# Two attention blocks on one core: an order of instructions laid out by a model of four engines, scores of four heads in one burst, transposes moved off the tensor engine, and a new start

## The chip, the cores and the metric

The kernel runs on one core of one Trainium2 chip. The metric is the device time in microseconds (us) of one execution on that core. Five engines work side by side, each through its own queue in program order: PE (tensor engine, matmuls), ACT (scalar engine, here the exponentials), DVE (vector engine), POOL and SP. SP does no arithmetic here; it issues all DMAs through one queue. PE's products go to PSUM, which both kernels lay out as eight banks of 512 f32 columns. To "evacuate" a bank is to copy it out, mostly by DVE, so that it can be used again. The "chain" of a profile is the work that ended last, followed back from wait to wait.

## The reference, cut to what matters

Two attention blocks read their own input of 2048 rows and 640 columns, and their outputs are put side by side. Both have 32 heads of 20 columns.

```python
# A: four segments of 512 rows; inside a segment causal attention, plus a memory M, z
for s in range(4):
    p = softmax(qs @ ks.T * 20 ** -0.5 + mask)          # per head
    a_dot = p @ vs
    a_mem = (phi(qs) @ M) / (phi(qs) @ z + 1e-6)        # phi(t) = t + 1 if t > 0 else exp(t)
    o = g * a_mem + (1 - g) * a_dot                     # g = sigmoid(beta), per head
    M = M + phi(ks).T @ vs;  z = z + phi(ks).sum(rows)
out_A = o @ wo
# B: sliding window, each row sees itself and the 255 rows before it
out_B = (softmax(q @ k.T * 20 ** -0.5, window 256) @ v) @ wo
```

Both kernels cut the work into eight chunks of 512 rows and run A0, B0, A1, B1, A2, B2, A3, B3. While one chunk's scores and exponentials run, the next chunk's q, k and v are projected.

## The kernel before

Four heads lie in four blocks of 32 partitions (20 used). A "slot" is one pair of heads and one block of keys and queries: two score matmuls on two row tiles of PE (a row tile is 32 of its 128 rows, used by itself), then one exp.

```python
    def bank(self):                                   # small PSUM banks: four
        return self.ps.tile([P, 512], F32, name="m", bufs=4)

    def scores(self, banks, b, pair, g, k, q, koff):  # L329, L336
        ps = self.ps.tile([P, 2, 512], F32, name="sc", bufs=2)
        for kt, q0, nq, c0 in banks[b]:
            for i in range(2):
                rows = slice(HD * (2 * pair + i), HD * (2 * pair + i) + HD)
                nc.tensor.matmul(ps[:, i, c0:c0 + nq * P], lhsT=k[rows, g, kc:kc + P],
                                 rhs=q[rows, g, q0 * P:(q0 + nq) * P], ...
                                 tile_position=(HD * (2 * pair + i), 0))
        nc.scalar.activation(out=pt[:, :, lo:hi], in_=ps[:, :, lo:hi], func=ACT.Exp, ...)
```

The product of probabilities and values (AV) comes out with the head's columns on partitions and has to be turned. DVE first copies it out of PSUM, PE turns it, DVE normalises. The finished rows are turned a second time for the output projection, again on PE.

```python
    def evac(self, O):                                # L409
        oc = self.wk.tile([P, 512], BF16, name="oc", bufs=4)
        self.nc.vector.tensor_copy(out=oc[:], in_=O[:])
    def turn(self, oc):                               # L415
        for b in range(LT):
            self.nc.tensor.transpose(out=t[:, b * P:(b + 1) * P],
                                     in_=oc[:, b * P:(b + 1) * P], identity=self.ident[:])
    def final_job(self, o_tok, b, wo, out_rows):      # L440 to L454
        for m in range(self.KT):
            nc.tensor.transpose(out=t[:, m * P:(m + 1) * P],
                                in_=o_tok[:, b, m * P:(m + 1) * P], identity=self.ident[:])
        nc.vector.tensor_copy(out=oT[:], in_=t[:, 0:self.KT * P])
        ...                                           # 2 x 5 matmuls with wo, copy, store
```

The next chunk's q and k take a round trip through memory so that heads land on blocks of 32 partitions: `st` is stored to scratch (`scr_qB<-st`), then read back by head ("spread", `qB<-scr_qB`). A class `Filler` hands out the projections between the slots by a credit that counts PE time only. The start fills large tiles with zeros on POOL while DVE computes the gate constants.

The softmax here doesn't subtract the row's maximum and nothing guards it: scores larger than these inputs give would overflow.

Of the kernel before, what the change touches and what calls it, by code (L numbers as in the profile page):

```python
# [2 lines left out]

# [5 lines left out]
ACT = mybir.ActivationFunctionType  # L9
# [13 lines left out]
VW = H * VS + 12  # L23
EPS = 1e-6

BANKS_A = [[(0, 0, 4, 0)], [(3, 3, 1, 0), (1, 1, 3, 128)], [(2, 2, 2, 0)]]
BANKS_B = [[(-2, 0, 1, 0), (0, 0, 3, 128)], [(2, 2, 2, 0), (-1, 0, 2, 256)],
           [(3, 3, 1, 0), (1, 1, 3, 128)]]
BANKS_B0 = [[(0, 0, 3, 128)], [(2, 2, 2, 0)], [(3, 3, 1, 0), (1, 1, 3, 128)]]
# [6 lines left out]
class Filler:  # L36

    def __init__(self, nslots):
        self.jobs = deque()
        self.nslots = nslots  # L40
        self.credit = 0.0

    def add(self, deadline, cost, gen):
        self.jobs.append([deadline, cost, gen])

    def step(self):
        job = self.jobs[0]
        try:
            c = next(job[2])
            job[1] = max(0.0, job[1] - c)  # L50
            return c
        except StopIteration:
            self.jobs.popleft()
            return 0.0

    def force(self, t):
        while any(j[0] <= t for j in self.jobs):
            self.credit -= self.step()

    def run(self, t, extra):  # L60
        total = sum(j[1] for j in self.jobs)
        rate = total / max(1, self.nslots - t)
        cum = 0.0
        for d, c, _ in self.jobs:
            cum += c
            rate = max(rate, cum / max(1, d - t))
        self.credit = min(self.credit + rate + extra, 1500.0)
        while self.jobs and self.credit > 0:
            self.credit -= self.step()

    def drain(self):
        while self.jobs:
            self.step()


class _K:

    def __init__(self, ctx, tc, S, D):
        self.ctx, self.tc, self.nc = ctx, tc, tc.nc
        self.S, self.D = S, D  # L80
        self.KT = D // P
        self.scale = float(DH) ** -0.5

# [9 lines left out]
    def bank(self):  # L93
        return self.ps.tile([P, 512], F32, name="m", bufs=4)

    def bank16(self):
        return self.ps.tile([P, 1024], BF16, name="m", bufs=4)
# [15 lines left out]
    def consts_masks(self):  # L113
        nc, cp = self.nc, self.cp
        self.zero = nc.gpsimd.to_reg(0.0)
        ident = cp.tile([P, P], BF16, name="ident")
        nc.gpsimd.memset(ident[:], 0.0)
        nc.gpsimd.affine_select(out=ident[:], in_=ident[:], pattern=[[-1, P]],
                                compare_op=ALU.not_equal, fill=1.0, base=0,
                                channel_multiplier=1)  # L120
        self.ident = ident
# [11 lines left out]
        self.rowmask = rowmask[:, 0:1]  # L133
        epsv = cp.tile([P, 1], F32, name="epsv")
        nc.vector.tensor_scalar(out=epsv[:], in0=rowmask[:],
# [17 lines left out]
    def consts_beta(self, beta):  # L153
        nc, cp = self.nc, self.cp
        b = cp.tile([P, H], BF16, name="beta")
        nc.sync.dma_start(out=b[:], in_=beta.rearrange("(o n) -> o n", o=1).to_broadcast([P, H]))
        e = cp.tile([P, H], F32, name="e32")
        nc.scalar.activation(out=e[:], in_=b[:], func=ACT.Exp, scale=-1.0)
        t = cp.tile([P, H], F32, name="t32")
        nc.vector.tensor_single_scalar(out=t[:], in_=e[:], scalar=1.0, op=ALU.add)  # L160
        r = cp.tile([P, H], F32, name="r32")
        nc.vector.reciprocal(out=r[:], in_=t[:])
        omg = cp.tile([P, H], F32, name="omg")
        nc.vector.tensor_tensor(out=omg[:], in0=e[:], in1=r[:], op=ALU.mult)
        self.omg = omg
        g8 = cp.tile([P, G], F32, name="g8")
        ev = e[:].rearrange("p (g j) -> p g j", j=4)
        for j in range(4):
            rows = slice(HD * j, HD * j + HD)
            nc.vector.tensor_copy(out=g8[rows, :], in_=ev[rows, :, j])  # L170
        self.g8 = g8

    def proj_direct(self, w, xT, dst, g, mask):
        nc = self.nc
        ps = self.bank()
        for kt in range(self.KT):
            for j in range(4):
                c0 = DH * (4 * g + j)
# [4 lines left out]
            yield mm_ns(512)  # L183
        if mask:
# [4 lines left out]
        yield 0.0  # L189

    def proj_compact(self, w_ap, xT, st, phi=None):
        nc = self.nc
        for m in range(self.KT):
            ps = self.bank()
            for kt in range(self.KT):
# [3 lines left out]
                yield mm_ns(512)  # L199
            nc.vector.tensor_copy(out=st[:, m, :], in_=ps[:, :])  # L200
            yield 0.0

    def spread(self, dst, src, c0, n, d0=0):
        for j in range(4):
            self.nc.sync.dma_start(
                out=dst[HD * j:HD * j + DH, :, d0:d0 + n],
                in_=src[:, c0:c0 + n].rearrange("(g j d) s -> j d g s", g=G, j=4)[j])

    def qk_job(self, w_ap, xT, scratch, col, dst, c0, n, d0=0):
        st = self.wk.tile([P, self.KT, L], BF16, name="st", bufs=2)  # L210
        yield from self.proj_compact(w_ap, xT, st)
        self.nc.sync.dma_start(
            out=scratch[:, col:col + L].rearrange("(m p) s -> p m s", p=P), in_=st[:])
        self.spread(dst, scratch, c0, n, d0)
        self.last_st = st
        yield 0.0

    def pq_job(self, scratch, dst):
        nc = self.nc
        st = self.last_st  # L220
        pc = self.wk.tile([P, self.KT, L], BF16, name="pqc", bufs=1)
        for m in range(self.KT):
            self.phi(pc[:, m, :], st[:, m, :])
            yield 250.0
        nc.sync.dma_start(out=scratch[:, :].rearrange("(m p) s -> p m s", p=P), in_=pc[:])
        self.spread(dst, scratch, 0, L)
        yield 0.0

    def phi(self, out, in_):
        nc = self.nc  # L230
        e = self.wk.tile([P, L], BF16, name="e", bufs=2)
        nc.scalar.activation(out=e[:], in_=in_, func=ACT.Exp)
        nc.vector.tensor_single_scalar(out=e[:], in_=e[:], scalar=1.0, op=ALU.min)  # L233
        nc.vector.scalar_tensor_tensor(out=out, in0=in_, scalar=0.0, in1=e[:],  # L234
                                       op0=ALU.max, op1=ALU.add)

    def pk_job(self, src, nt, pkT):
        nc = self.nc
        pend = None
        for i in range(nt + 1):  # L240
            if i < nt:
                pk = self.wk.tile([P, L], BF16, name="pk", bufs=2)
                self.phi(pk[:], src[:, i, :])
                yield 250.0
            if pend is not None:
                pi, ppk = pend
                pt = self.bank16()
                for b in range(LT):
                    nc.tensor.transpose(out=pt[:, b * P:(b + 1) * P],
                                        in_=ppk[:, b * P:(b + 1) * P],  # L250
                                        identity=self.ident[:])
                yield 4 * mm_ns(128)
                nc.vector.tensor_copy(
                    out=pkT[:, :, pi * P:(pi + 1) * P],
                    in_=pt[:, 0:LT * P].rearrange("p (b c) -> p b c", b=LT))
                yield 0.0
            pend = (i, pk)

    def dm_job(self, seg, pkT, coloff, v):
        nc = self.nc  # L260
        dM = self.bank()
        dv = dM[:, 0:G * HD].rearrange("p (g c) -> p g c", c=HD)
        for g in range(G):
            for kt in range(LT):
                for j in range(4):
                    h = 4 * g + j
                    rows = slice(HD * j, HD * j + HD)
                    nc.tensor.matmul(dv[rows, g, 0:VS],
                                     lhsT=pkT[:, kt, coloff(h):coloff(h) + HD],
# [3 lines left out]
                yield 4 * 27.0  # L273
# [8 lines left out]
        self.mz = mz  # L282
        MZ = self.wk.tile([P, G, HD], BF16, name="MZ", bufs=2)
# [5 lines left out]
        self.MZ = MZ  # L289
        yield 0.0  # L290

    def v_job(self, w_ap, xT, v, gate):
        nc = self.nc
        for tt in range(LT):
            for hf in range(2):
                ps = self.bank()
                for kt in range(self.KT):
# [3 lines left out]
                    yield mm_ns(320)  # L301
# [10 lines left out]
                yield 0.0  # L312

    def v_tile(self, name, n):
        out = []
        for i in range(n):
            v = self.big.tile([P, LT, VW], BF16, name="%s%d" % (name, i))
            self.nc.gpsimd.memset(v[:], 1.0)
            out.append(v)
        return out  # L320

    def scores(self, banks, b, pair, g, k, q, koff):
        nc = self.nc
        ps = self.ps.tile([P, 2, 512], F32, name="sc", bufs=2)
        for kt, q0, nq, c0 in banks[b]:
            for i in range(2):
                rows = slice(HD * (2 * pair + i), HD * (2 * pair + i) + HD)
                kc = P * (kt + koff)
                nc.tensor.matmul(ps[:, i, c0:c0 + nq * P], lhsT=k[rows, g, kc:kc + P],  # L329
                                 rhs=q[rows, g, q0 * P:(q0 + nq) * P],  # L330
                                 start=True, stop=True,
                                 tile_position=(HD * (2 * pair + i), 0))
        lo = min(e[3] for e in banks[b])
        hi = max(e[3] + e[2] * P for e in banks[b])
        pt = self.wk.tile([P, 2, 512], BF16, name="pt", bufs=12)
# [347 lines left out]
```

## Time and profile before

| before | |
|---|---|
| median (range, runs) | 530.2 us (527.1 to 531.0, 16) |
| span of the profiled run, granted PE clock | 528.5 us, 0.906 |
| first matmul, first exp | 8.9 us, 27.4 us |
| end of the last exp, end | 509.5 us, 528.5 us |
| chunks, first exp to first exp | 63.3, 63.2, 54.0, 71.1, 54.2, 73.2, 54.2, 48.8 us |

Four lines of the page: the DMA queue (packets, MB, share of the time of 16 DMA engines), and the groups of exps and scores (line, engine, operation, output<-input, shapes, count | busy us, mean ns of one | idle time of that engine just before them, and what ended most of it).

```profile
q1 hardware_dynamic: 52136, 40.32, 28.3%
...
L336 ACT ACTIVATE pt<-sc 128x1024 bf16<-128x1024 f32 (+2 forms) x384 | 346.4, 929 | 128.6 <-PE sc L329 115.6
...
L329 PE MATMUL sc<-qB,kB 32*128 32x128 bf16 (+2 forms) x704 | 79.5, 303 | 8.8 <-ACT pt L336 8.0
L329 PE MATMUL sc<-qA,kA 32*128 32x128 bf16 (+3 forms) x512 | 67.7, 304 | 14.9 <-DVE qA L188 14.3
```

The DMA engines are busy for little more than a quarter of the time. Score matmuls hold PE for 79.5 + 67.7 = 147 us of busy time, and ACT stands idle for 128.6 us in front of its exps.

### The profile page before, as it was taken

The page shows a single profiled execution, that of the slowest core. Times are in us where ns is not written, and L with a number is a line of the kernel's source. Part 1 is how long each engine was busy: PE and PEld are TensorE (multiplying, and loading weights), DVE is VectorE, ACT ScalarE, POOL GpSimd, SP SyncE. Part 2 cuts the span into 40 slices and gives each one's busy share as a digit, 9 for nine tenths or more (in the row PEclk, how much of TensorE's full clock was granted, in tenths as well). Part 3 has the DMA queues.
Part 4 walks back from the last instruction along what each step waited for, and adds up shares of the span by engine and source line. Part 5 has one row for each costly group of instructions (what it writes and reads, how often), then busy time and mean ns, then how long its engine had stood idle before and what let it go on. Part 6 is the DMA issues. An engine that isn't in the chain of part 4 may idle for free.

```text
span 528.5 us, 11841 instructions
## 1 busy us (share of the span) xinstructions
PE 451.8 (85%) x4781; PEld 202.1 (38%) x4806; DVE 331.3 (63%) x690; ACT 364.7 (69%) x419; POOL 261.0 (49%) x530
## 2 busy tenths in 40 slices
PE   3099998699798999969899899878979899899965
PEld 0043334333244334434344334433334433444433
DVE  0845555845656767766666677775674677766643
ACT  0046678667787777867878677775877777879950
POOL 9623344356564344635555344544544444468850
PEclk9689999569799999968979999995987999979988
DMA  8900234103541154100563035300262105301101
GB/s 244 344 8 2 51 98 112 42 2 92 157 101 39 43 143 104 39 14 2 151 146 80 27 100 125 74 29 1 76 154 71 40 14 125 100 14 38 39 14 50
DMA packets 52191, 41.07 MB, mean 78 GB/s; under 512 B 22440, under 2 KB 51496, under 8 KB 52136
## 3 DMA queue, kind: packets, MB, share of 16 engines
q1 hardware_dynamic: 52136, 40.32, 28.3%
q8 instruction: 37, 0.61, 0.5%
q14 instruction: 18, 0.15, 0.1%
HBM read 18.69 MB, written 16.38 MB: 66 GB/s over the span
## 4 chain that ended last, share of the span: by engine, by line
PE 70%; DVE 14%; ACT 7%; issue 3%; POOL 0%; POOLq 0%; ACTq 0%; DVEq 0%
PE sc L329 18%; PE m L196 15%; PE m L298 9%; PE m L450 9%; PE m L391 8%; ACT pt L336 6%; PE m L415 4%; PE m L179 3%; DVE oT L444 2%; DVE pk L234 2%; DVE ot L454 2%; DVE oc L409 1%; DVE pqc L234 1%; DVE e L233 1%; PE m L403 1%
## 5 line engine op out<-in xcount | busy, mean ns | idle before, releaser
L336 ACT ACTIVATE pt<-sc 128x1024 bf16<-128x1024 f32 (+2 forms) x384 | 346.4, 929 | 128.6 <-PE sc L329 115.6
L342 POOL TENSOR_SCALAR_AFFINE_SELECT pt<-pt 128x256 bf16<-128x256 bf16 (+1 forms) x336 | 165.9, 497 | 215.6 <-ACT pt L336 213.9
L348 POOL TENSOR_SCALAR_AFFINE_SELECT pt<-pt 128x256 bf16<-128x256 bf16 x176 | 81.2, 463 | 33.0 <-ACT pt L336 33.0
L409 DVE CAST oc<-m 128x512 bf16<-128x512 f32 x88 | 58.5, 688 | 55.7 <-PE m L391 54.2
L329 PE MATMUL sc<-qB,kB 32*128 32x128 bf16 (+2 forms) x704 | 79.5, 303 | 8.8 <-ACT pt L336 8.0
L329 PE MATMUL sc<-qA,kA 32*128 32x128 bf16 (+3 forms) x512 | 67.7, 304 | 14.9 <-DVE qA L188 14.3
L200 DVE CAST st<-m 128x512 bf16<-128x512 f32 x70 | 48.1, 688 | 26.3 <-PE m L196 23.9
L196 PE MATMUL m<-xT,wB 128*128 128x512 bf16 x185 | 51.6, 381 | 1.6 <-issue 1.0
L454 DVE CAST ot<-m 128x320 bf16<-128x320 f32 x64 | 31.3, 489 | 29.9 <-PE m L450 29.3
L329 PEld LDWEIGHTS <-kA 32*128 32x128 bf16 x512 | 19.2, 91 | 73.0 <-issue 55.5
L329 PEld LDWEIGHTS <-kB 32*128 32x128 bf16 x704 | 22.9, 94 | 58.5 <-issue 53.0
L450 PEld LDWEIGHTS <-oT 128*128 128x128 bf16 x320 | 26.2, 100 | 40.4 <-DVE oT L444 21.3
L450 PE MATMUL m<-wo_B,oT 128*128 128x320 bf16 x160 | 31.2, 322 | 8.2 <-DVE oT L444 7.8
L298 PEld LDWEIGHTS <-xT 128*128 128x128 bf16 x320 | 28.2, 105 | 22.5 <-issue 11.7
L450 PE MATMUL m<-wo_A,oT 128*128 128x320 bf16 x160 | 31.1, 302 | 6.3 <-DVE oT L444 6.3
L298 PE MATMUL m<-wv_A,xT 128*128 128x320 bf16 x160 | 35.8, 363 | 0.0
L415 PE MATMUL m<-ident,oc 128*128 128x128 bf16 x352 | 32.6, 230 | 3.6 <-DVE oc L409 3.6
L362 DVE TENSOR_TENSOR pt<-pt,fdmask 128x512 bf16<-128x512 bf16 x48 | 21.9, 457 | 19.0 <-ACT pt L336 18.4
L429 DVE TENSOR_TENSOR o_tok<-m,rr 128x320 bf16<-128x320 bf16 x64 | 31.5, 492 | 2.2
L391 PE MATMUL m<-pt,vB 128*32 128x384 bf16 (+2 forms) x704 | 29.2, 301 | 1.9 <-POOL pt L348 1.9
L298 PE MATMUL m<-wB,xT 128*128 128x320 bf16 x160 | 28.4, 301 | 0.0
L426 DVE RECIPROCAL rr<-m 128x16 f32<-128x16 bf16 x88 | 22.2, 252 | 8.2 <-PE m L415 7.3
(68 smaller groups left out, 417.0 us busy)
## 6 DMA issues: line engine op xcount, KB each, us to landing
out_dram<-ot SPq DMA_DIRECT2D x32, 160.0 KB
kB<-scr_kB SPq DMA_DIRECT2D x12, 240.0 KB
scr_kB<-st SPq DMA_DIRECT2D x4, 640.0 KB
scr_qB<-st SPq DMA_DIRECT2D x4, 640.0 KB
qB<-scr_qB SPq DMA_DIRECT2D x16, 160.0 KB
wB<-in_B_wqkv_dram SPq DMA_DIRECT2D x1, 2400.0 KB
scr_kA<-st SPq DMA_DIRECT2D x3, 640.0 KB
kA<-scr_kA SPq DMA_DIRECT2D x12, 160.0 KB
```

The lines of the kernel that those rows point to most:

```text
L196: nc.tensor.matmul(ps[:, :], lhsT=w_ap[:, kt, m * P:(m + 1) * P], rhs=xT[:, kt, :], start=(kt == 0), stop=(kt == self.KT - 1))
L200: nc.vector.tensor_copy(out=st[:, m, :], in_=ps[:, :])
L298: nc.tensor.matmul(ps[:, 0:320], lhsT=xT[:, kt, tt * P:(tt + 1) * P], rhs=w_ap[:, kt, 320 * hf:320 * hf + 320], start=(kt == 0), stop=(kt ...
L329: nc.tensor.matmul(ps[:, i, c0:c0 + nq * P], lhsT=k[rows, g, kc:kc + P], rhs=q[rows, g, q0 * P:(q0 + nq) * P], start=True, stop=True, tile ...
L336: nc.scalar.activation(out=pt[:, :, lo:hi], in_=ps[:, :, lo:hi], func=ACT.Exp, scale=self.scale)
L342: self.nc.gpsimd.affine_select(out=blk, in_=blk, pattern=[[0, 2 * n], [1, P]], compare_op=ALU.is_ge, fill=self.zero, base=0, channel_multi ...
L348: self.nc.gpsimd.affine_select(out=blk, in_=blk, pattern=[[0, 2], [-1, P]], compare_op=ALU.is_ge, fill=self.zero, base=-1, channel_multipl ...
L391: nc.tensor.matmul(O[HD * j:HD * j + HD, q0 * P:(q0 + nq) * P], lhsT=v[:, vt, VS * h:VS * h + HD], rhs=pts[(b, j // 2)][:, j % 2, c0:c0 + ...
L409: self.nc.vector.tensor_copy(out=oc[:], in_=O[:])
L415: self.nc.tensor.transpose(out=t[:, b * P:(b + 1) * P], in_=oc[:, b * P:(b + 1) * P], identity=self.ident[:])
L450: nc.tensor.matmul(ps[:, 0:320], lhsT=oT[:, m * P:(m + 1) * P], rhs=wo[:, m, 320 * hf:320 * hf + 320], start=(m == 0), stop=(m == self.KT ...
L454: nc.vector.tensor_copy(out=ot[:, 320 * hf:320 * hf + 320], in_=ps[:, 0:320])
```

## The change

The change has four parts. The second and the third take work off PE; the first lays out the order so that all engines are fed.

1. **Order.** `Filler` goes. A class `Flow` keeps a clock for PE, ACT, DVE and POOL while the program is built, with a duration for each kind of instruction, and at each step issues what its model says is ready. As with `Filler`, the order is fixed once the program is built; nothing is decided on the chip.
2. **Scores.** Four heads in one burst on four row tiles, into two score tiles. Three score tiles (six banks) in place of two, so two small banks in place of four. Half-width blocks of A are joined in pairs (384 exps become 352).
3. **Transposes.** AV is turned by DVE straight out of PSUM, in blocks of 32x32, with no copy before. Heads are regrouped (h = 8j + g) so that this gives rows. The turn for the output projection becomes four stores to scratch and one transposing DMA back. The keys for the memory go the same way. The last chunk multiplies its padded heads by a padded weight instead, with the evacuation shared between ACT and DVE.
4. **Start.** Zero fills on DVE as 32-bit words, the gate constants later.

```diff
-class Filler:
-    ...                       # credit per slot, counts PE time only
+class Flow:
+    def __init__(self):
+        self.pe = self.act = self.dve = self.pool = 0.0
+        self.bank_free = [0.0, 0.0]
+    def on_pe(self, mode, ns, ready=0.0):
+        if mode != self.mode:
+            ns += 110.0       # another tile shape
+            self.mode = mode
+        self.pe = max(self.pe, ready) + ns
+        return self.pe
+    ...
     def bank(self):
-        return self.ps.tile([P, 512], F32, name="m", bufs=4)
+        f.pe = max(f.pe, f.bank_free.pop(0))
+        return self.ps.tile([P, 512], F32, name="m", bufs=2)
...
-        ps = self.ps.tile([P, 2, 512], F32, name="sc", bufs=2)
-        for kt, q0, nq, c0 in banks[b]:
-            for i in range(2):
+        ps = [self.ps.tile([P, 2, 512], F32, name="sc", bufs=NSC) for _ in range(2)]   # NSC = 3
+        for g, kt, q0, nq, c0 in ent:
+            for j in range(4):
...
-    def evac(self, O):
-        oc = self.wk.tile([P, 512], BF16, name="oc", bufs=4)
-        self.nc.vector.tensor_copy(out=oc[:], in_=O[:])
-    def turn(self, oc):
-        for b in range(LT):
-            self.nc.tensor.transpose(...)
+    def turn(self, O, tt, i):
+        self.nc.vector.transpose(out=tt[:, i, :], in_=O[:, :])
...
     def final_job(...):
-        for m in range(self.KT):
-            nc.tensor.transpose(...)
-        nc.vector.tensor_copy(out=oT[:], in_=t[:, 0:self.KT * P])
+        for j in range(4):
+            nc.sync.dma_start(
+                out=scr[:, GW * j:GW * (j + 1)].rearrange("(b t) c -> t b c", t=HD),
+                in_=o[HD * j:HD * (j + 1), :, :])
+        yield t + 4500.0
+        oT = self.big.tile([P, self.KT, L], BF16, name="oT", bufs=2)
+        nc.sync.dma_start_transpose(out=oT[:], in_=scr[:, :])
+        yield max(t + 4500.0, f.pe) + (14000.0 if n < 7 else 6000.0)
...
-        nc.gpsimd.memset(qB[:], 0.0)
-        nc.gpsimd.memset(kB[:], 0.0)
+        nc.vector.memset(self.qB[:].bitcast(F32), 0.0)
+        nc.vector.memset(self.kB[:].bitcast(F32), 0.0)
```

## The prediction

> **What bounds the kernel now.** I read the page first: busy shares, chain, then the waits.
>
> ```profile
> PE 451.8 (85%) x4781; PEld 202.1 (38%) x4806; DVE 331.3 (63%) x690; ACT 364.7 (69%) x419; POOL 261.0 (49%) x530
> ...
> PE 70%; DVE 14%; ACT 7%; issue 3%; POOL 0%; POOLq 0%; ACTq 0%; DVEq 0%
> ```
>
> The tensor engine (PE) carries 70% of the chain that ended last, the scalar engine (ACT) only 7%. The list of waits (total us, times, longest) says who waits for whom:
>
> ```profile
> ACT pt L336 <- PE sc L329: 115.6, 198, 13.2
> ...
> PE sc L329 <- DVE qA L188: 14.3, 2, 13.5
> ...
> PE sc L329 <- ACT pt L336: 8.0, 13, 1.7
> ```
>
> ACT waits 115.6 us for scores; PE waits 8.0 us for ACT. So PE is the bound between start and tail. The timeline of PE alone (start, duration, ..., count) shows how it spends itself:
>
> ```profile
> 200.18 0.85 PE L298 MATMUL m<-wB,xT 128*128 128x320 bf16 x5
> 200.97 0.39 PE L329 MATMUL sc<-qA,kA 32*128 32x512 bf16 x2
> 201.29 0.85 PE L298 MATMUL m<-wB,xT 128*128 128x320 bf16 x5
> ...
> 203.50 0.73 PE L391 MATMUL m<-pt,vA 128*32 128x512 bf16 x16
> 204.16 0.40 PE L403 MATMUL m<-pqA,MZ 32*32 32x512 bf16 x4
> ```
>
> Durations overlap, so I count from start to start. Five 320-column matmuls take 0.79 us (200.18 to 200.97); inside such a run the step is 0.136 us (320 columns at 2.4 GHz plus 2.5 ns), five are 0.68, so about 0.1 us goes to the change to another tile shape. Two 512-column score matmuls on two row tiles take 0.32 us: 0.213 once (they run side by side) plus 0.1. Sixteen L391 matmuls (four heads, 1280 columns each) take 0.66 us, 0.53 plus 0.1: four column tiles do run side by side.
>
> The ends: the first scores wait, and the last exp is at 509.5 of 528.5 us.
>
> ```profile
> 14.26 7.61 DVE L160 TENSOR_SCALAR t<-e 128x32 f32<-128x32 f32 x1 [11.95 <-ACT e L158]
> 18.32 3.51 POOL L488 MEMSET pqA<- 128x4096 bf16 x1
> ...
> 26.75 0.62 PE L329 MATMUL sc<-qA,kA 32*128 32x512 bf16 x4 [13.54 <-DVE qA L188]
> ...
> 524.98 0.49 DVE L454 CAST ot<-m 128x320 bf16<-128x320 f32 x1 [0.19 <-PE m L450]
> ```
>
> A 32-element vector (DVE) instruction took 7.61 us and ends with the pool engine's memset (21.87 against 21.83 us), with the first evacuations queued behind it.
>
> **What the Trainium skill says.** "TensorEngine Tiling (Array Packing)", Key Properties: changing the tiling mode drains the engine. The trace agrees, about 0.1 us a change. "TensorE: Matmul & The Clock Gate", Measured speedup vs the span model: four 32-row tiles run together, 3.07 times faster measured, each a few ns behind the other. The trace shows it for four column tiles and for pairs of row tiles; four row tiles no run shows yet. "Advanced Engine Details and Errata", Mode Summary: the second vector port is shared with GpSimd and the two block each other. The 7.61 us above fits. "VectorE: DVE Perf Modes", The three transpose paths: the vector transpose works in 32x32 blocks only; its time for 128x512 from PSUM no run shows. I take that of the evacuation of equal size, 0.69 us long, 0.60 to 0.61 from start to start when back to back.
>
> **The change part by part.** I counted PE instructions in the program order of both kernels and priced them start to start: columns/2.4 ns plus 2.5, divided by the tiles side by side, plus 0.1 us per change of tile shape.
>
> Scores: four heads in one burst over two score buffers, where there were two. 1216 matmuls stay; 77 us become 40. PE transposes go: 352 (L415), 160 (L440) and 72 (L249) at 0.056 us are 33 us. Their work moves to DVE (32x32 blocks out of PSUM, 88 times), and to transposing DMAs through DRAM (7 outputs, 3 keys). The last chunk instead multiplies padded heads by a padded weight: output projection 43.5 becomes 46.7 us. Changes of tile shape: 789 become 415, 79 us become 41. All else on PE (projections, values, AV, memory: 185 us) stays. PE floor: 417 before, 314 after, **103 us less**.
>
> ACT: the half-width score blocks of A are joined, 384 exps become 352. A run of 15 full exps took 13.86 us, so 0.92 each; 320 x 0.92 + 16 x 0.71 + 16 x 0.50 + 33 x 0.52 = 331 us, plus 1.4 for four copies in the tail: 332, about as before. So ACT, now waiting, becomes the longer of the two.
>
> DVE: evacuation of oc, copies to oT and pkT go (88 x 0.60 + 32 x 0.40 + 18 x 0.33 = 72 us), 88 transposes (53) and 8 in the tail come, normalisation takes about as long as before. 331 busy become about 280.
>
> PE and ACT limit different chunks, so I cut both orders at the chunk boundaries. In us, PE/ACT: A0 55/41, B0 35/39, A1 35/37, B1 41/49, A2 36/37, B2 39/47, A3 41/37, B3 33/46. The larger of each pair sums to **350 us**.
>
> Start: the first matmul came at 8.92 us, waiting for weights, and does not move. The wait of 13.5 us should vanish: the large zero memsets leave POOL for DVE in uint32 form, ahead of the first evacuations, and the beta constants run late. Add about 4 us for the cold clock (five 512-column steps took 0.43 us each at the start instead of 0.22). Tail: 19 us after the last exp become about 10, by my sum: mask 0.4, AV 0.7, transpose to transpose on DVE 1.9, some 30 matmuls of 0.14 = 4, evacuation 0.5, last store 3 (525.5 to 528.5 now).
>
> Sum without losses: 8.9 + 4 + 350 + 10 = 373.
>
> Losses: before, PE's floor without the tail is about 408 us and the stretch from first matmul to last exp, less the start wait, 487: a factor of 1.19. The clock row has a mean of 0.906, that is about 100 us at half speed, 15 of it at the start; where PE is the bound those cost some 43 us; without them the factor is 1.09. The slow windows lie where PE does transposes and waits for DVE (0.66 in 88 to 118 us); without PE transposes I expect few. I take 1.08 on 350, 28 us: **about 402 us**.
>
> **The rivals.** (1) *ACT bubbles.* Three score buffers hold one and a half bursts: burst i+1 can start only when the first exp of burst i is done, and must be written within the 0.92 us of the second. An AV of 0.7 us in the way starves ACT. For: queues are in program order, so a drift is not made good. Against: PE steps are 0.14 to 0.22 us and the order was laid out with durations that the trace confirms. 0.3 us on half of 176 bursts is 26 us: 400 with little else, 425 with DVE stalls. (2) *DVE as the bound.* The small PSUM pool shrinks from four banks to two, and every projection, AV and memory product needs one. For: 280 us of DVE in 390 is 72%, and norms now read two SBUF operands, contending with POOL. Against: PE waited 0.6 us only for oc with four banks, and DVE is below 80% in any chunk by count. It would make 430 to 450. (3) *DMA round trips late.* Queries and keys went from store to first use in about 10.5 us (79.85 to 90.3); the last projection of the next chunk is 10 to 19 us of PE work before the boundary. Added output round trips share the one in-order queue. A miss of 3 us at each of seven boundaries is 21 us: 420. (4) *Nothing gained*, if four row tiles don't overlap: 37 us back on PE, which then sets nearly every chunk: 420 to 430.
>
> **Range and chances.** 374 is the sum without losses; 432 is factor 1.08 plus one rival in full. I say 402, range 374 to 432. Even two rivals together stay below 470, far under 530, so faster by over 2%: 0.97, within 2%: 0.02, slower: 0.01.
>
> **What would show it right or wrong.** Right: PE busy near 330 to 350 us and ACT near 360 (durations, not steps); ACT's share above 85%; ACT large in the chain; first exp before 16 us; no wait of PE on DVE above 15 us in sum; the four score matmuls of an entry starting within 20 ns. Wrong: a wait of PE for DVE evacuations or transposes of 30 us or more (rival 2), scores waiting for DMA at chunk boundaries (3), score bursts of 0.5 us (4), DVE transposes well above 0.7 us, or granted clock below 0.85 in the body.

## The result, and the profile after

| | before | after |
|---|---|---|
| median (range, runs) | 530.2 us (527.1 to 531.0, 16) | 423.3 us (417.5 to 426.0, 9) |
| ratio of the fast runs | | 0.7964, 95% interval 0.7937 to 0.7992 |
| busy PE / ACT / DVE / POOL | 452 / 365 / 331 / 261 us | 356 / 339 / 308 / 253 us |
| first exp | 27.4 us | 15.9 us |
| first exp to end of last exp | 482.1 us | 392.4 us |
| end of last exp to end | 19.0 us | 14.8 us |
| time at half of the full PE clock, first exp to end of last exp | 81 us | 64 us |

Every ratio in this document is the mean time of one kernel's fast runs over the mean of the kernel before's fast runs from the same rounds on the same chip, so it is not quite the ratio of the medians quoted. The profiled run of after took 424.8 us. It counts as slow, because it lies more than 1.5% (1.7%) above the fastest of the nine, but this kernel spreads by 2% without a gap, so I read it as the upper end of its range and draw nothing from it that rests on less than a few us. The time of a run is about 1.7 us longer than the span in its profile.

The three rows before the last add up the gain of 105.4 us in the span: 11.5 us in the start, 89.7 in the body, 4.2 in the tail.

The page of after first: busy shares, the DMA queue, the chain that ended last by engine, and the groups that answer those of before.

```profile
PE 355.7 (84%) x4213; PEld 162.6 (38%) x4246; DVE 307.8 (73%) x599; ACT 339.1 (80%) x391; POOL 252.6 (60%) x496
...
q1 hardware_dynamic: 95512, 54.25, 52.5%
...
PE 45%; DVE 20%; ACT 13%; DMA 12%; issue 5%; POOL 2%; SPq 2%; ACTq 0%; DVEq 0%; POOLq 0%
...
L433 ACT ACTIVATE pt<-sc 128x1024 bf16<-128x1024 f32 (+1 forms) x352 | 321.8, 1023 | 56.1 <-PE sc L421 55.1
...
L505 DVE STREAM_TRANSPOSE tt<-m 128x512 f32<-128x512 f32 x88 | 60.9, 707 | 19.4 <-PE m L484 18.7
...
L421 PE MATMUL sc<-qB,kB 32*128 32x384 bf16 (+2 forms) x704 | 48.5, 298 | 21.5 <-ACT pt L433 16.7
...
L421 PE MATMUL sc<-qA,kA 32*128 32x128 bf16 (+3 forms) x512 | 36.7, 310 | 4.9 <-ACT pt L433 4.8
```

The same 1216 score matmuls now hold PE for 48.5 + 36.7 = 85 us, 62 less than before. One score matmul takes as long as before (about 300 ns); there are four in flight where there were two. ACT's idle time in front of its exps fell from 128.6 to 56.1 us. PE's share of the chain fell from 70% to 45%: DVE and DMA carry a third of it, and DMA, not named in the chain before, has 12%. The DMA queue moved nearly twice the packets and is busy for over half of the time.

The list of waits of after (total us, times, longest) says what is left:

```profile
ACT pt L433 <- PE sc L421: 55.1, 46, 5.8
...
PE sc L421 <- ACT pt L433: 21.5, 36, 1.7
...
PE sc L421 <- DMA qB<-scr_qB: 4.2, 5, 1.1
```

ACT waited 198 times before and 46 times now, but each wait is longer (1.2 us in the mean against 0.6). Those are not mainly the small bubbles between bursts: the 31 waits under 1 us sum to 13 us. Five stalls of 3 to 6 us, at 25 us (in A0), 71 (ahead of B0), 120 (early in A1), 257 (ahead of B2) and 357 (ahead of B3), make up 23.6 of the 55.1 us. The timeline of the boundary into B2 shows one (start us, duration us, engine, line, operation, count, and in brackets the idle time before and what ended it).

```profile
254.82 1.53 SPq L252 DMA_DIRECT2D qB<-scr_qB  x4
255.02 1.94 ACT L433 ACTIVATE pt<-sc 128x1024 bf16<-128x1024 f32 x2 [0.18 <-PE sc L421]
...
258.16 0.21 PE L421 MATMUL sc<-qB,kB 32*128 32x128 bf16 x1 [0.69 <-DMA qB<-scr_qB]
...
261.78 0.37 PE L421 MATMUL sc<-qB,kB 32*128 32x128 bf16 x5 [0.89 <-DMA qB<-scr_qB]
...
262.22 1.94 ACT L433 ACTIVATE pt<-sc 128x1024 bf16<-128x1024 f32 x2 [5.26 <-PE sc L421]
```

ACT has done the last exps of A2 at 256.96 us. The first scores of B2 need the queries of four head blocks, which four DMAs bring; they were issued only at 254.82 and land one after the other until 261.7. The wait is booked on PE for DMA with 0.7 to 1.1 us each, on ACT for PE with 5.26 us. The view of waits alone would name PE.

The chunks, cut at the first exp of each, tell where the body's time went (us; the floors are those of the prediction, the larger of its PE and ACT sums; the last column is an experiment told below).

| chunk | before | after | floor predicted | after, without the transposing DMA of the output |
|---|---|---|---|---|
| A0 | 63.3 | 58.5 | 55 | 58.5 |
| B0 | 63.2 | 43.4 | 39 | 43.0 |
| A1 | 54.0 | 45.2 | 37 | 39.6 |
| B1 | 71.1 | 54.8 | 49 | 53.9 |
| A2 | 54.2 | 44.2 | 37 | 39.9 |
| B2 | 73.2 | 48.7 | 47 | 47.3 |
| A3 | 54.2 | 51.7 | 41 | 50.0 |
| B3 | 48.8 | 45.7 | 46 | 46.1 |
| sum | 482.1 | 392.4 | 350 | 378.3 |

B2 and B3 lie within 2 us of their floors, which are ACT's, B0 and B1 4 to 6 us above theirs. The chunks of A lie 3.5 to 11 us above theirs.

### The profile page after: what moved, and what is told of

Its sections match the earlier page's. It is cut to its first block, busy times and chain, and to the rows that moved or that the text cites. A ratio compares the mean times of both kernels' runs of the same rounds, so it can differ in the third digit from the quotient of the medians.

```text
span 423.1 us, 10639 instructions
## 1 busy us (share of the span) xinstructions
PE 355.7 (84%) x4213; PEld 162.6 (38%) x4246; DVE 307.8 (73%) x599; ACT 339.1 (80%) x391; POOL 252.6 (60%) x496
## 3 DMA queue, kind: packets, MB, share of 16 engines
q1 hardware_dynamic: 95512, 54.25, 52.5%
## 4 chain that ended last, share of the span: by engine, by line
PE 45%; DVE 20%; ACT 13%; DMA 12%; issue 5%; POOL 2%; SPq 2%; ACTq 0%; DVEq 0%; POOLq 0%
PE m L240 15%; ACT pt L433 12%; PE sc L421 8%; PE m L484 6%; PE m L573 5%; DMA scr_qB<-st 5%; DVE tt L505 4%; PE m L386 4%; PE m L215 4%; DVE st L247 4%; DMA qB<-scr_qB 3%; DVE u L539 2%; PE sc L885 2%; DMA out_dram<-ot 2%; DVE ot L579 1%
## 5 line engine op out<-in xcount | busy, mean ns | idle before, releaser
L433 ACT ACTIVATE pt<-sc 128x1024 bf16<-128x1024 f32 (+1 forms) x352 | 321.8, 1023 | 56.1 <-PE sc L421 55.1
L471 POOL TENSOR_SCALAR_AFFINE_SELECT pt<-pt 128x512 bf16<-128x512 bf16 (+1 forms) x304 | 174.7, 576 | 135.3 <-ACT pt L433 132.9
L505 DVE STREAM_TRANSPOSE tt<-m 128x512 f32<-128x512 f32 x88 | 60.9, 707 | 19.4 <-PE m L484 18.7
L421 PE MATMUL sc<-qB,kB 32*128 32x384 bf16 (+2 forms) x704 | 48.5, 298 | 21.5 <-ACT pt L433 16.7
L421 PE MATMUL sc<-qA,kA 32*128 32x128 bf16 (+3 forms) x512 | 36.7, 310 | 4.9 <-ACT pt L433 4.8
L240 PEld LDWEIGHTS <-wB 128*128 128x128 bf16 x200 | 17.9, 102 | 30.1 <-issue 17.6
L484 PE MATMUL m<-pt,vA 128*32 128x256 bf16 (+3 forms) x512 | 24.7, 316 | 2.0 <-DVE st L247 1.0
L484 PEld LDWEIGHTS <-vB 128*32 128x32 bf16 x704 | 17.6, 102 | 16.6 <-issue 9.2
L421 PEld LDWEIGHTS <-kA 32*128 32x128 bf16 x512 | 10.5, 92 | 33.5 <-issue 32.5
L539 DVE TENSOR_TENSOR u<-tt,rr 128x640 bf16<-128x640 f32 x24 | 22.2, 926 | 0.5
```

Source lines behind the costliest of these rows:

```text
L240: nc.tensor.matmul(ps[:, :], lhsT=w_ap[:, kt, m * P:(m + 1) * P], rhs=xT[:, kt, :], start=(kt == 0), stop=(kt == self.KT - 1))
L421: nc.tensor.matmul(ps[j // 2][:, j % 2, c0:c0 + nq * P], lhsT=k[rows, g, kc:kc + P], rhs=q[rows, g, q0 * P:(q0 + nq) * P], start=True, sto ...
L433: nc.scalar.activation(out=pt[:, :, lo:hi], in_=ps[i][:, :, lo:hi], func=ACT.Exp, scale=self.scale)
L471: nc.gpsimd.affine_select(out=blk, in_=blk, pattern=pat, compare_op=ALU.is_ge, fill=self.zero, base=0, channel_multiplier=-1)
L484: nc.tensor.matmul(O[HD * j:HD * j + HD, q0 * P:(q0 + nq) * P], lhsT=v[:, vt, VS * h:VS * h + HD], rhs=pts[j // 2][:, j % 2, c0:c0 + nq * ...
L505: self.nc.vector.transpose(out=tt[:, i, :], in_=O[:, :])
```

## The experiments

The theory after the result, D where an expectation uses a letter, was that the gain is what was counted, and that the 21 us between 402 and 423 come mostly from the memory round trips of the output, which share one queue and the DMA engines with the hand-over of q and k. Its rivals were that one engine's busy time sets the pace, and that PSUM buffers do, with too few score tiles or too few small banks. Twelve kernels ran. No run has the transposes or the new order alone, so how the gain in the body divides between them and the bursts is argued from the counting and not shown.

### b_start: the kernel before with the new start alone

```diff
-        self.consts_beta(A_beta)
+        self.load_beta(A_beta)          # the constants themselves after the first evacuations
-        nc.gpsimd.memset(qB[:], 0.0)
-        nc.gpsimd.memset(kB[:], 0.0)
+        nc.vector.memset(qB[:].bitcast(F32), 0.0)
+        nc.vector.memset(kB[:].bitcast(F32), 0.0)
```

> The kernel before with the start of the change alone: the zero memsets of qB and kB on the vector engine in 4-byte form, and the beta constants computed just ahead of the first value projection. Theory of the prediction (the 13.5 us wait at the start is on the path and nothing else takes its place): first exp at about 16 us instead of 27.4, and the whole 11 to 13 us come off, 517 to 520 us. Rival (chunk A0 is bound by PE work and weights that arrive late, so the gain at the start is given back): first exp early, but 525 us or more.

Measured: 516.1 us against 528.8 of before in the same rounds, ratio 0.9758 (0.9713 to 0.9802). The first exp came at 14.8 us instead of 27.4, and every chunk after it took what it took before (63.5, 63.3, 54.0, 71.1, 54.3, 73.2, 54.2, 48.8). The start part is worth 12.7 us by itself, and all of it is kept; that is a little more than the theory expected, and its rival falls.

### b_burst4: the kernel before with bursts of four heads alone

```diff
+        if pair == 0:                   # both pairs at once; still two score tiles, four small banks
+            self.burst = [self.ps.tile([P, 2, 512], F32, name="sc", bufs=2) for _ in range(2)]
-            for i in range(2):
+                for j in range(4):
...
+        ps = self.burst[pair]
```

> The kernel before with four-head score bursts alone, with its own buffers (two score buffers, four small banks), so a burst fills both buffers. Theory (PE is the bound; the scores' share of it falls from 77 to 40 us and some 190 bursts each save two changes of tile shape where they stood apart): 470 to 490 us. Rival (without a third score buffer PE has to wait for both exps before each burst and gives it back): 505 us or more, with a wait of PE on ACT of 40 us or more.

Measured: 528.95 us, ratio 1.0008 (0.9957 to 1.0060). A look at the page's busy line and at the waits of this run:

```profile
PE 412.6 (78%) x4781; PEld 204.2 (39%) x4806; DVE 327.6 (62%) x690; ACT 351.5 (67%) x419; POOL 260.4 (49%) x530
```

```profile
ACT pt L338 <- PE sc L330: 127.0, 125, 13.4
PE sc L330 <- ACT pt L338: 46.4, 100, 2.9
```

The theory's 470 to 490 us failed and its rival came true. PE's busy time fell by 39 us (451.8 before), and the kernel gained nothing: PE's waits for ACT rose from 8.0 to 46.4 us. With two score tiles a burst fills both, so the next can be finished only after both exps are done, and ACT then has nothing to do while PE writes. PE's time was saved and given back as a new wait. (A version with three score tiles and two small banks could not be tried: the old order holds a bank open across other products, and by my notes it deadlocked before it got to a chip.)

### a_nsc2_m4: after with two score tiles and four small banks

```diff
-NSC = 3
+NSC = 2
-        self.bank_free = [0.0, 0.0]
+        self.bank_free = [0.0] * 4
-        return self.ps.tile([P, 512], F32, name="m", bufs=2)
+        return self.ps.tile([P, 512], F32, name="m", bufs=4)
-                    need = [self.sc_free[2 * i - 2] + 60.0 if i else 0.0]
+                    need = [self.sc_free[2 * i - 1] + 60.0 if i else 0.0]
...                                           # and the tail's third accumulator in small banks
```

> The changed kernel with two score buffers and four small banks instead of three and two, order laid out anew. Theory S (the third score buffer is what lets ACT run without bubbles): each of 176 bursts waits for both exps before it, some 0.4 to 0.5 us of ACT idle each in the chunks where ACT has no slack, 450 us or more. Theory V (small banks are short): 420 or less.

Measured: 485.2 us, ratio 0.9142 (0.9119 to 0.9165), 62 us slower than after. The busy line and the waits of this run:

```profile
PE 390.2 (81%) x4246; PEld 172.1 (36%) x4246; DVE 308.7 (64%) x599; ACT 349.4 (72%) x391; POOL 250.8 (52%) x496
```

```profile
ACT pt L433 <- PE sc L421: 100.3, 128, 4.3
PE sc L421 <- ACT pt L433: 69.9, 94, 1.2
```

Both engines now wait for one another, 100 and 70 us. So the third score tile is what makes the burst pay, even in the new order, and two small banks are a good price for it: the exchange as a whole costs 62 us. It does not say that four small banks by themselves are of no use, since both numbers were changed at once; chunk A0 took 54.4 us here and 58.5 in after. Two reservations. The order is laid out anew for these sizes, so it is not the same program with other buffers. And the granted PE clock was 0.838 here and 0.923 in after, and PE was busy for 34 us more with the same matmuls; whether the lower clock follows from the waits or makes a part of the 62 us by itself is not shown.

### a_pe_dup, a_act_dup, a_dve_dup: work added to one engine at a time

```diff
# a_pe_dup: the first entry of each burst is computed twice
-        for g, kt, q0, nq, c0 in ent:
+        for g, kt, q0, nq, c0 in ent[:1] + ent:
# a_act_dup: one small exp more per burst
+            if i == 1:
+                nc.scalar.activation(out=self.junk[:], in_=self.fd[:, 0:64], func=ACT.Exp)
# a_dve_dup: each reciprocal of the normalisation twice
             nc.vector.reciprocal(out=rr[:, 0:nm, :], in_=tv[:, 0:nm, :, DH])
+            nc.vector.reciprocal(out=rr[:, 0:nm, :], in_=tv[:, 0:nm, :, DH])
```

The model in `Flow` is told nothing of the added work.

> The changed kernel with the first entry of each four-head score burst multiplied twice (about 18 us more PE time over all chunks, same results, order laid out with the old costs). If PE still set the pace throughout, 18 us would come on, 438 or more. Theory D (chunks A are held by PE together with DMA, chunks B by ACT with PE slack, by the floors 10 us on average): 429 to 436.

> The changed kernel with a small extra exp of 64 columns ahead of every second score exp (176 of them, 0.12 us each from start to start, about 21 us of ACT). If ACT sets the pace in chunks B only (96 of 176 bursts), 11 to 14 us come on, 433 to 437; if it sets it everywhere, 20 or more; if score buffers are the limit (a burst waits for the first exp of the one before), more than 21, since each delay is passed on to the next burst.

> The changed kernel with the reciprocal of each head group done twice (64 more vector instructions, about 16 us, same results). Theory V (the vector engine with two small banks holds chunks A): 12 us or more, 434 and up. Theory D: the vector engine has slack of a quarter, 2 to 7 us come on, 425 to 430.

| run | busy time added | median us | ratio to before (95%) | longer than after |
|---|---|---|---|---|
| a_pe_dup | PE 355.7 to 373.2: 17.5 us | 429.6 | 0.8100 (0.8046 to 0.8155) | 7.2 us |
| a_act_dup | ACT 339.1 to 361.8: 22.7 us | 432.6 | 0.8143 (0.8114 to 0.8173) | 9.5 us |
| a_dve_dup | DVE 307.8 to 324.6: 16.8 us | 428.1 | 0.8084 (0.8051 to 0.8117) | 6.4 us |

The last column is the difference of the ratio from 0.7964, times 530 us. Each engine passes on about 0.4 of what is added to it (0.2 to 0.6, with the intervals). The first and the last came out as theory D expected, a_act_dup a little under its 433 to 437. In a_act_dup PE, to which nothing was added, was busy for up to 11.6 us more (33 of after's matmul records are missing) at a granted clock of 0.913 (0.923 in after), so not all of its 9.5 us need be ACT's. None of the three sets the pace alone, and none is free: the rival of the single engine falls for them. POOL, busy for 60%, was not loaded. The chain of the kernel before was PE's by 70%; here three engines share the pace.

### a_no_o_dma: after without the output's round trip (wrong result)

```diff
-        for j in range(4):
-            nc.sync.dma_start(out=scr[:, GW * j:GW * (j + 1)]..., in_=o[HD * j:HD * (j + 1), :, :])
-        nc.sync.dma_start_transpose(out=oT[:], in_=scr[:, :])
+        oT = self.oT0                   # a constant tile; all products stay
```

> The changed kernel without the output's round trip through DRAM (no store of o, no transposing DMA; the output product reads a constant tile, so the result is wrong on purpose); same instruction order on all compute engines. Theory D (added DMA traffic delays queries, keys and output stores in the one in-order queue; that is what the A chunks lose): the store of q lands in 3 to 4 us again instead of up to 10, ACT idles of 4 to 5 us at 119.8 and 257 us go, total 403 to 412 us. Theory V (the vector engine with two small banks sets the pace of the A chunks): 417 us or more.

Measured: 407.2 us, ratio 0.7703 (0.7672 to 0.7735). That is 16.2 us less than after (0.7964 - 0.7703 = 0.0261, or 13.8 us, by the ratios). A1 and A2 take 39.2 and 39.9 us. The theory holds: most of the missing time is the round trip's.

### a_no_oT: only its transposing half left out (wrong result)

```diff
-        oT = self.big.tile([P, self.KT, L], BF16, name="oT", bufs=2)
-        nc.sync.dma_start_transpose(out=oT[:], in_=scr[:, :])
+        oT = self.oT0                   # the four stores of o stay
```

> Half of the output round trip taken out: the four stores of o to scratch stay in every chunk but the last, the transposing DMA that reads them back is left out, and the products take a constant tile (wrong result on purpose, as in a_no_o_dma). Taking out the whole round trip gave 407.2 us against 423.3. If the transposing DMAs (their traffic and the 2.4 to 5.7 us that each issue holds the SP queue) are what costs, this run comes to 406-412 us, ratio about 0.77, with the store of q of B1 (chunk A1) landing within 5 us. If the stores (some 14,000 packets of 320 bytes, written in the same stretch as the q and k hand-over) are what costs, it stays at 417-424, ratio 0.79 or above. Halfway, 412-417, says that both take part.

Measured: 409.9 us, ratio 0.7703 (0.7673 to 0.7733), the same as without the whole round trip. The order of instructions on PE, DVE and ACT is that of after; seven issues are missing on SP and one memset on POOL is new. The products with wo no longer depend on the DMA, but in after no wait of PE for it is on the list either. The stores keep their 14,784 packets (77,368 here, 62,584 in a_no_o_dma) and cost at most 3 us. The seven transposing DMAs cost 13.5 us by the medians, 13.8 by the ratios.

How, the timelines tell. A1 shortens from 45.2 to 39.6 us, and the stall of 4.65 us early in it is gone. It begins 20 us earlier, in B0, where a chunk's output leaves. SP in after, then in this run:

```profile
91.33 2.93 SPq L558 DMA_DIRECT2D scr_o<-o  x4
98.75 2.59 SPq L565 DMA_TRANSPOSE oT<-scr_o  x1
101.43 0.53 SPq L257 DMA_DIRECT2D scr_qA<-st  x1
...
119.07 1.05 SPq L582 DMA_DIRECT2D out_dram<-ot  x2
```

```profile
91.14 2.86 SPq L558 DMA_DIRECT2D scr_o<-o  x4
94.10 1.77 SPq L257 DMA_DIRECT2D scr_qA<-st  x1
...
114.50 1.05 SPq L581 DMA_DIRECT2D out_dram<-ot  x2
```

After its stores of o, SP holds the transposing DMA back until they have landed (4.4 us, by the queue's own waits), and issuing it takes 2.6 us. The store of A1's queries stands behind it in the same queue and is issued at 101.4 in place of 94.1. What follows is late in turn, down to the stores of finished output rows, 4.6 us later (119.07 against 114.50). Those hold the row buffers, and the three lines under a_ot5 below show DVE, PE and ACT stopped for 4 us by them.

A2 shortens from 44.2 to 39.9 us, and here it is the stall ahead of B2 shown above, 5.26 us of ACT, of which 0.94 is left. SP in after, then in this run, from the store of B2's keys on:

```profile
231.53 0.39 SPq L257 DMA_DIRECT2D scr_kB<-st  x1
...
239.46 2.65 SPq L565 DMA_TRANSPOSE oT<-scr_o  x1
242.22 1.65 SPq L252 DMA_DIRECT2D kB<-scr_kB  x4
244.71 0.39 SPq L257 DMA_DIRECT2D scr_qB<-st  x1
```

```profile
224.06 0.39 SPq L257 DMA_DIRECT2D scr_kB<-st  x1
...
228.63 2.37 SPq L252 DMA_DIRECT2D kB<-scr_kB  x4
237.25 0.39 SPq L257 DMA_DIRECT2D scr_qB<-st  x1
242.50 1.49 SPq L252 DMA_DIRECT2D qB<-scr_qB  x4
```

The read-back of the keys is issued 10.7 us after their store in after, behind the transposing DMA, and 4.6 us after it in this run. So in after the keys' read-back, the transposing DMA and the store of the queries run together, and the store's read-back can be issued only 10.1 us later (254.82, in the lines above), against 5.3 us here. The difference, 4.9 us, fits the 4.3 us by which ACT's stall shrank. The same lateness occurs ahead of B1 (9.8 us against 4.2), where it costs ACT only 0.3 us: those queries had been projected early enough.

The stall of 5.8 us ahead of B3 is in this run too, and so are those in A0 and ahead of B0. In the chain through the one ahead of B3, PE and DVE take turns and no DMA appears. In A0, PE works through 6 us of projections that the order puts between two bursts (23.14 to 29.26 us in after). Ahead of B0, 20 value products took 4.84 us in a stretch of half clock, 0.24 us each, where five took 0.84 just after.

The time at half clock between first and last exp is shorter without the transposing DMAs, 46 us (48 in a_no_o_dma) against 64. Whether this follows from the shorter waits or gives a part of the gain by itself is not shown. A2 has none of it in either run, and A1 3.4 us in after and none here, so the clock explains nothing of A2's gain and at most 1.7 us of A1's.

### a_ot5: five output row buffers in place of three

```diff
-            ot = self.wk.tile([P, 640], BF16, name="ot", bufs=3)
+            ot = self.wk.tile([P, 640], BF16, name="ot", bufs=5)
```

> The changed kernel with five buffers for output rows instead of three. Theory D in the part that runs over output stores (vector engine waited 6.4 us for a store to free a row buffer, PE 3.9 us behind it at 118 us, since only two small banks are there): 3 to 6 us less, 415 to 419. Theory V: within 1 us of the changed kernel.

Measured: 419.3 us, ratio 0.7898 (0.7840 to 0.7956), with the very same order of instructions. It is aimed at the end of the first of these two paths, the stall early in A1 of after:

```profile
121.51 0.89 DVE L579 CAST ot<-m 128x320 bf16<-128x320 f32 x2 [3.94 <-DMA out_dram<-ot]
122.06 1.80 PE L240 MATMUL m<-xT,wB 128*128 128x512 bf16 x4 [3.92 <-DVE ot L579]
...
124.49 1.02 ACT L433 ACTIVATE pt<-sc 128x1024 bf16<-128x1024 f32 x1 [4.65 <-PE sc L421]
```

DVE waits for a store to free a row buffer, PE for DVE to free a bank, ACT for PE: one late store stops three engines for 4 us. With five buffers the stall is gone from its place, and one of 3.2 us comes 11 us later. A1 takes 43.4 us, against 45.2 in after and 39.6 without the transposing DMAs, so the row buffers by themselves give back less than half of A1's loss. Two more buffers bring 4.0 us by the medians and 3.5 by the ratios, but the intervals touch, so that they help is likely and not shown.

### a_late_o, a_late_ot5, a_late_want_ot5: the output's round trip issued later

These try to keep the round trip and take it out of the way: a chunk's output is stored and turned only after the next chunk's queries are handed over. The second adds five row buffers, the third also hurries the projections of q and k (done by 75% of a chunk, not 90%).

```diff
# final_job, ahead of the stores of o
+        if n < 6:
+            yield self.known(n + 2, "q", extra=-9500.0)
+            t = max(t, f.pe)
# a_late_ot5, a_late_want_ot5
-            ot = self.wk.tile([P, 640], BF16, name="ot", bufs=3)
+            ot = self.wk.tile([P, 640], BF16, name="ot", bufs=5)
# a_late_want_ot5
-            want = min(1.0, (i - first[n]) / (0.9 * count[n]))
+            want = min(1.0, (i - first[n]) / (0.75 * count[n]))
```

> The changed kernel with the output's round trip (store of o, transposing DMA) issued only when the next chunk's queries have been handed to their load; right results, same traffic, another order. Theory D, if the harm is that the round trip sits ahead of the queries in the queue: the store of q in chunk A1 lands in 3 to 5 us instead of 9.8, half or more of the 15 us that leaving the round trip out gained comes back, 408 to 417. If it is the traffic as such, 420 to 426.

> The same with five output row buffers: if the two gains are apart (queue order, store waits), 3 to 5 us below the run with the late round trip alone, 405 to 413; if both are the same congestion, no further gain.

> The same with the next chunk's query and key products finished by 75% of a chunk instead of 90%, so that they land before the chunk ends. If the 5.8 us of ACT idle before chunk B3 and the like come from too late a product, 3 to 8 us less than with five buffers; if chunks A lack PE time rather than notice, no change or some us more.

| run | median us | ratio to before (95%) | A1, A2, A3 us |
|---|---|---|---|
| after | 423.3 | 0.7964 (0.7937 to 0.7992) | 45.2, 44.2, 51.7 |
| a_late_o | 435.9 | 0.8209 (0.8172 to 0.8247) | 45.9, 51.0, 60.1 |
| a_late_ot5 | 424.6 | 0.8014 (0.7983 to 0.8046) | 45.9, 53.1, 47.1 |
| a_late_want_ot5 | 433.2 | 0.8143 (0.8089 to 0.8197) | 42.3, 60.0, 43.8 |

None is better. The first came out of both ranges; the second gained 11.3 us on it where 3 to 5 were expected, and the third took 8.6 us more than the second, the other branch of its expectation. The part that I wanted did happen: in A1 of a_late_o the store of the queries landed in 4.3 us (issued at 151.41, read-back at 155.66). But laid out anew, the order had issued that store 5.5 us later than after did (145.91), so nothing was gained. And the late outputs piled up: in the waits of a_late_o DVE stands 10.7 us at one time for an output store, and PE 10.4 us behind it.

Five row buffers take that stall away, and A2 still takes 53 us. There one stall of ACT is 9.2 us long (16.3 in a_late_want_ot5): in PE's order the next scores stand behind 31 (65) output products and projections and behind memory products that wait 2.1 (3.3) us for the read-back of phi(q). The clock fell to half only in the later part of these stalls, so it did not start them; it may have lengthened what followed, with 19 (27) us of A2 at half clock and none in after. Moving work in a fixed order moves everything around it, so these three runs show that this way round is no cure; they do not weigh the two parts of the cost against each other, the time that the transposing DMA holds the queue and its packets among the others'. That stays open, as does a second queue for it, which was not tried.

No version with right results beat after beyond its interval; a_ot5 comes nearest.

## Why the prediction was right or wrong

The time was right: 423 us lies in the range of 374 to 432, at its upper end, and faster by over 2% was given 0.97. By its own steps:

**Start: right.** The forecast was that the wait of 13.5 us vanishes. The first exp came 11.5 us sooner and before 16 us, and b_start shows the part by itself with 12.7 us. The sum had 8.9 + 4 = 12.9 us for it and 15.9 were measured. That the shared port of DVE and POOL made the 32-element instruction slow fits, and was not tested by itself: b_start also moved the constants away, and the section that the prediction cites says it of vector instructions that use both ports, which no run shows for this one.

**Scores: right.** Four row tiles overlap, so rival 4 falls. The four matmuls of an entry start mostly 3 to 4 ns apart. In the PE timeline of after a 512-column entry is followed like this:

```profile
137.86 0.39 PE L421 MATMUL sc<-qA,kA 32*128 32x512 bf16 x4
138.19 1.04 PE L240 MATMUL m<-xT,wB 128*128 128x512 bf16 x4
```

Four heads take 0.33 us, shape change included, where two took 0.32. What the counting did not say is that this saving is worth nothing alone. b_burst4 saved 39 us of PE and gained 0; a_nsc2_m4 lost 62 us. The third score tile was named in the prediction under rival 1 as a danger, as too few; by these two runs it is what makes the part work. Rival 1 itself is small: PE waits 21.5 us for ACT, and ACT's waits under 1 us sum to 13 us.

**PE, ACT and DVE busy: nearly right.** PE's 356 us are just above 330 to 350. ACT's 339 are below 360, and near the 332 that the prediction had as a sum of steps: busy time counts overlapping exps once, and ten in a row took 9.27 us, 0.93 each, as priced. The price of a matmul, columns/2.4 ns plus 2.5, fits the trace of before, where one follows the other in 56, 136 and 216 ns at 128, 320 and 512 columns. DVE's 308 are above 280. The 88 transposes carry 8 of these 28 us (60.9 us busy, priced at 53), at 707 ns each and 0.63 to 0.65 us from start to start back to back (priced at 690 ns and 0.60 us); the rest of DVE's list was undercounted by 20. Two sums of the prediction are off by little: the larger floors as printed add up to 351, and the items of PE's saving to 105, not 103. "ACT's share above 85%" failed with 80%, and ACT has only 13% of the chain. The picture of ACT as the new bound holds for B2 and B3 alone. Elsewhere three engines share the pace, as the three added loads show.

**Rival 2, DVE and the two small banks: in part.** "No wait of PE on DVE above 15 us in sum" failed, with about 20 us over all rows of the list. It did not reach the 30 us that would have been a bound, and the largest single stall in it comes from a store that a row buffer waits for, so from DMA. That DVE stays below 80% in any chunk failed narrowly, with 82% in B0 and 83% in B1. Four small banks were tried only together with two score tiles.

**Losses: the mis-sized term.** The prediction took a factor of 1.08 on 350 us, 28 us, and kept the late round trips as a rival that would make 420. First exp to last exp took 392.4 us, 42 over the floor. Without the seven transposing DMAs it takes 378.3, 28 over the floor: the factor's number fits everything else, and rival 3 came true on top of it, with 13.5 us. That the number fits is in part luck. It was taken from the kernel before by leaving the slow clock out, because few slow windows were expected without PE transposes. That step failed: after still has 64 us at half clock between first and last exp (81 before), 46 without the transposing DMAs, so the 28 us need not be the losses that the factor was taken from. (The sign set for it, a clock below 0.85 in the body, did not come: 0.92.) Rival 3 was not at each of seven boundaries with 3 us, as imagined, but mostly in A1 and A2 (5.6 and 4.3 us), and only in A2 by queries that came late; in A1 the stall stood at the row buffers, though five of them gave back only 1.8 us of A1's 5.6. The reasoning saw "the one in-order queue" and did not price what a wait at its head costs all that stands behind.

**Tail: mis-sized.** 14.8 us came in place of 10. In the timeline, item by item of the prediction's list: 2.9 until AV starts (0.4 forecast), because it stands behind 24 output products in PE's order that run until 411.2 us though the masks are done at 409.7; AV 0.9; transposes 2.3; 5.3 for the products (4 forecast), which wait three times for ACT to finish an evacuation; evacuation 0.5; store 2.9. The 24 products took 0.20 us each, partly at half clock (399 to 409 us); at the usual 0.136 they would have ended with the masks, so the clock is a rival to the order here, and untested.

From the forecast to the profiled run: 401 (8.9 + 4 + 350 + 28 + 10) + 3 (start) + 14 (transposing DMAs) + 5 (tail) = 423, the span; the time of the run is 2 us longer.

## What to carry to other kernels

Work saved on the engine that bounds counts only if its consumer can keep up and there is room for the result: before making bursts twice as wide, give the buffer between the two engines one more slot, and look for the saving in the opposite wait if it does not show. A transpose taken off an engine and given to DMA is not free because the DMA engines are idle on average: ask what stands behind it in the queue, and how long before a chunk boundary. When three engines each pass on 0.4 of what is added to them, no single one of them is the bound, and much of what remains is in a few long stalls, found in the timeline rather than in the sums. And compare the granted clock of two runs before giving their difference to the edit.

## What the Trainium skill lacked or had wrong

- "TensorEngine Tiling (Array Packing)", Key Properties, says that a change of tiling mode drains the engine and gives no cost. Here a change costs about 0.1 us (0.33 us from the start of a 512-column entry on four row tiles to the next shape, of which 0.21 us are columns). The change removed 374 of 789 such changes.
- "VectorE: DVE Perf Modes", The three transpose paths, gives a vector transpose for 128x128 bf16 only. Here 128x512 took 0.71 us, the same in f32 out of PSUM and in bf16 out of SBUF.
- "Advanced Engine Details and Errata", X-Bar Transpose (TRN2), says that transposing DMAs are as fast as regular ones. Here they took 1.4 times as much of the DMA engines: by differences between runs, the seven cost 454 engine-us for 4.59 MB (52.5% of 16 x 423.1 us less 47.4% of 16 x 408.7), and the 28 plain stores of the same bytes 319 (47.4% less 42.7% of 16 x 407.0). On the queue the gap is wider: each held SP's queue for 2.4 to 3.9 us at issue, a plain store of the same size 0.4, and seven of them cost 13.5 us of 423. That section doesn't speak of it.
